# Normalised attention and a low-rank mixer on one core: the first batch staged by neighbouring heads, with 64x64 turnings and another written order

## The chip, the cores and the metric

The kernel runs on one core of a Trainium2 chip, as one program. The metric is the device time in microseconds (us) of one execution. Five engines work beside each other, each through its own list of instructions in a fixed order: TensorE (PE; its weight loads are shown apart as PEld), VectorE (DVE), ScalarE (ACT), GpSimd (POOL) and SyncE (SP), which here only issues transfers. An instruction starts when the one before it on its engine lets it, and when the semaphores that it waits for have come.

## What is computed

There are 8 batches of 12 heads, 448 positions and 64 numbers per head, and a two-layer mixer with 768 columns and a hidden width of 3072. Cut to what matters:

```
q_n, k_n = rmsnorm(q, g_q), rmsnorm(k, g_k)          # x / sqrt(mean(x*x) + 1e-6) * g
scores   = q_n @ k_n.T / sqrt(64)
attn     = exp(scores - max) / (sum + 1e-9)
x        = (attn @ v) laid out as [batch, 448, 768]
h        = x.T @ U @ V                               # rank 32, over the positions
u        = x + h.T
out      = u + relu(u @ w_ch1) @ w_ch2
```

All inputs and the output are float32; the kernel multiplies in bfloat16.

## The kernel before, in words

**Tiling.** The 12 heads of a batch are worked in three groups of four heads, so there are 24 groups (`groups`, L76). The 448 positions are cut into 7 blocks of 64 (`NT`). A group's queries and keys lie in SBUF as `qf` and `kf`, 128 partitions by 14 rows of 64 numbers: two heads share the partitions (64 each), and the index c = 0, 1 in the free direction gives the other two. A pair of heads is worked together through the scores, their exponentials and the products with the values; a batch has six pairs.

**Norms.** For each group the squares of `qf` and `kf` are taken (ACT or POOL), summed on DVE into `ssq`, and turned into reciprocal roots on ACT by a logarithm and an exponential (`rs`, or `rp` where the result goes to PSUM for DVE). A multiplication by them on DVE or POOL gives `qn` and `kp` in bfloat16.

**Turning.** The scores need queries and keys with the 64 numbers of a head on the partitions. In groups 0 to 5 TensorE does it, seven 128x128 transposes for q and seven for k (`turn`, L363), into PSUM tiles `pt`. `take_q` (L371) copies a pair's queries to `qT` times the gain `gg`; `take_k` (L380) copies the keys to `kT` in three copies: 128x384 for the first six blocks and two of 64x64 for the last. `kT` has 512 columns; in its last 128 the two heads' keys stand in a diagonal of 64x64 blocks with zeros beside them (`fill_keys`, L260), so that one matmul gives the last scores of both heads. From group 6 on, DMA transposes do this.

**Pairs.** In most groups a pair is heads 0 and 2, or 1 and 3, of the group, which is how a whole 128x128 transpose leaves them. Only group 2 (`BESIDE`, L83) is loaded so that neighbours make a pair; each of its q and k loads is then two transfers of 64 partitions (L97).

**Scores, exponentials, products.** For a pair, `scores` (L418) fills four tiles: three of 128x896 (two heads by 448) and one of 128x448, from a pool of two PSUM buffers. `exps` (L433) turns each into `E` on ACT. `products` (L490) multiplies E with the values for half of the rows, and `norms` (L507) divides on DVE into `x`.

**Mixer.** `mix_t0` and `mix` (L644, L654) add the low-rank part of batch 0 and turn it to `uT`. `up_one` (L706, matmuls on L711) makes the first four tiles of the hidden layer in single steps, `up` (L689, matmuls on L693) the others, six matmuls each, `down` (L733, matmuls on L740) the second layer. The weights come in float32 from HBM and are cast to bfloat16 by POOL's transfers: `w1b` in four pieces (hidden tiles 0 to 3, 4 to 9, 10 to 15, 16 to 23; L295) and `w2b` in eight (L303).

**The order.** The first batch is ordered by hand: the string `FRONT` (L897) names steps in the order in which they are put into the engines' lists. A step is a short name with its numbers, and after a colon the engine (a for ACT, v for DVE, p for POOL). `S.0.1` is score tile 1 of pair 0, `E.0.1` its exponential, `V.0.1` the products of its second half, `N` the division, `turn`, `tq` and `tk` the turning and the copies, `sq`, `sm`, `rt`, `sc` the four steps of the norms, `val` the casting of a group's values (after it stands `load` of the group three later), `w` one piece of weights, `b.22` 22 matmuls on an identity whose result nobody uses (`keep_busy`, L242; 72 of them stand at the very start), `mt`, `mtc`, `mix`, `mc` and `u` the mixer. Before, the first norms of group 0 go in two parts of three or four blocks (`sqp`, `smp`, `rt0`, `scp`; `PARTS` are blocks 0 to 3 and 4 to 6). Behind the front, a planner (L1050) mixes the attention of the later batches with the mixer by estimated costs that begin at zero there.

**Transfers.** SP's list of loads begins with q and k of groups 0 and 1, q of group 2, v of group 0, k of group 2, v of group 1, then U, V, v of group 2. In the built program each transfer of SP and ACT waits for the landing of the one eight places earlier in their common order. POOL's transfers, the weights, are a queue of their own.

**Buffers.** The small PSUM tiles (`pt`, `rp`, `pv`, `busy`, `pu`, `ph`, `pg`) share four buffers; a step that takes one waits for the last reader of the tile that was there.

Of the kernel before, what the change touches and what calls it, by code (L numbers as in the profile page):

```python
# [9 lines left out]
FP32 = mybir.dt.float32  # L10
BF16 = mybir.dt.bfloat16
# [16 lines left out]
def kernel(  # L28
# [19 lines left out]
    P = 128  # L48
# [34 lines left out]
    BESIDE = 2  # L83
# [22 lines left out]
    def load_v(gi, eng=None):  # L106
        b, h0, n = groups[gi]
        t = staged[gi][2]
        toks = v[b, h0:h0 + n].rearrange("h (p j) d -> p h (j d)", j=NT)
        for i in range(2):  # L110
            (eng or nc.sync).dma_start(
                t[i * R:(i + 1) * R, :NM, :].rearrange("p (h j) d -> p h (j d)", j=NJ),
                toks[:, :, i * NJ * D:(i + 1) * NJ * D])
        for e in range(2):
            hs = slice(e, 4, 2) if gi == BESIDE else slice(2 * e, 2 * e + 2)
            (eng or nc.sync).dma_start(t[e * R:(e + 1) * R, NM:, :], toks[:, hs, 2 * NJ * D:])
# [30 lines left out]
    def squares_part(i, lo, hi, eng):  # L147
        if (0, i) not in sqs:
            sqs[(0, i)] = normp.tile([P, 2 * NT, D], FP32, name="sq", tag="sq")
        sq, x = by_c(sqs[(0, i)])[:, :, lo:hi, :], by_c(staged[0][i])[:, :, lo:hi, :]  # L150
        if eng is None:
            nc.scalar.activation(sq, x, AF.Square)
        else:
            eng.tensor_mul(sq, x, x)

    def sums_part(i, lo, hi):
        nc.vector.tensor_reduce(ssqs[0][:, i, :].rearrange("p (c j) -> p c j", c=2)[:, :, lo:hi],
                                by_c(sqs[(0, i)])[:, :, lo:hi, :], AX, ALU.add)

    def scale_part(i, lo, hi, eng):  # L160
        eng.tensor_tensor(
            normed[0][i].rearrange("p j c d -> p c j d")[:, :, lo:hi, :], by_c(staged[0][i])[:, :, lo:hi, :],
            rss[0][:, i].rearrange("p (c j) -> p c j ()", c=2)[:, :, lo:hi, :].to_broadcast([P, 2, hi - lo, D]),
            ALU.mult)
# [61 lines left out]
    PARTS = ((0, 4), (4, NT))  # L226
    for i in range(2):
        load_qk(0, i)
# [5 lines left out]
    load_qk(2, 0)  # L234
    load_v(0)
    load_qk(2, 1)
# [29 lines left out]
    fill_keys(0, nc.vector)  # L266
    for e in range(2):
        nc.gpsimd.tensor_mul(gp[:, e * D:(e + 1) * D], grow[:, 0, :], grow[:, 1, :])
# [76 lines left out]
    def fill_mixer():  # L345
        nc.gpsimd.memset(Uz, 0.0)
        fill_values(2, nc.gpsimd)
        fill_keys(1, nc.gpsimd)
# [14 lines left out]
    def turn(gi, i):  # L363

        pt = pts[(gi, i)] = ps.tile([P, NT, 2, R], BF16, name="pt", tag="ps")
        pos = POS_ODD if i == 0 and groups[gi][0] % 2 else POS
        for j in (*range(*PARTS[1]), *range(*PARTS[0])) if gi == 0 else range(NT):
            nc.tensor.transpose(pt[:, pos[j]].rearrange("p a r -> p (a r)"),  # L368
                                normed[gi][i][:, j].rearrange("p c d -> p (c d)"), ident)

    def take_q(gi, a, scalar=False):  # L371
        qT = q_bufs[gi % 2][:, a]
        dst, src = qT.rearrange("p (j r) -> p j r", r=R), pts[(gi, 0)][:, :, a, :]
# [6 lines left out]
    def take_k(gi, a):  # L380
        src = pts[(gi, 1)][:, :, a, :]
        kT = kT_bufs[gi % 2][:, a]
        nc.vector.tensor_copy(kT[:, :SM].rearrange("p (j r) -> p j r", r=R), src[:, :2 * NJ])
# [106 lines left out]
    def products(b, pr, half):  # L490
# [4 lines left out]
        first_h, step = (2 * lp, 1) if gi == BESIDE else (lp, 2)  # L495
# [11 lines left out]
    def norms(b, pr, half):  # L507
        gi, lp = divmod(b * NPAIR + pr, 2)
        first_h, step = (2 * lp, 1) if gi == BESIDE else (lp, 2)
# [360 lines left out]
    for b in range(B):  # L870
# [36 lines left out]
        u.2.1 V.5.1 N.5.0 rt.3 u.3.0 u.3.1 N.5.1 u.0.3 u.1.3 u.2.3 u.3.3 mt.3 u.0.2 mix.4 mtc.3 u.1.2 mix.5 mc.4:a u.2.2 u.3.2  # L907
        mc.5:a u.0.4 u.1.4 u.2.4 u.3.4 u.0.5 u.1.5 u.2.5 u.3.5
# [4 lines left out]
    def square_of(gi, i, eng):  # L913
        eng = None if eng is nc.scalar else eng
        squares(gi, i, eng, beside if (gi, i) == (2, 0) else None)

    placed = {t.partition(":")[0]: t.partition(":")[2] for t in FRONT.split()}
    rps = {}

    def root_of(gi, i, name):  # L920
        if placed.get(name) != "v":
            return rss[gi][:, i]
        if gi not in rps:
            rps[gi] = ps.tile([P, 2, 2 * NT], FP32, name="rp", tag="ps")
        return rps[gi][:, i]

    def part(t, p):
        lo, hi = PARTS[p]
        return t.rearrange("p (c j) -> p c j", c=2)[:, :, lo:hi]

    def roots_in(gi):
        if gi not in rss:
            rss[gi] = normp.tile([P, 2, 2 * NT], FP32, name="rs", tag="rs")
        return rss[gi]

    def log_part(i, p):
        nc.scalar.activation(part(roots_in(0)[:, i], p), part(ssqs[0][:, i], p), AF.Ln, scale=1.0 / D, bias=eps)

    def root_part(i, p):
        nc.scalar.activation(part(root_of(0, i, f"scp.{i}.{p}"), p), part(rss[0][:, i], p), AF.Exp, scale=-0.5)  # L940

    def log_of(gi, i=None):
        h = slice(0, 2) if i is None else slice(i, i + 1)
        nc.scalar.activation(roots_in(gi)[:, h], ssqs[gi][:, h], AF.Ln, scale=1.0 / D, bias=eps)

    def root(gi, i=None):
        if i is None and placed.get(f"sc.{gi}.0") == placed.get(f"sc.{gi}.1"):
            root_of(gi, 0, f"sc.{gi}.0")
            dst = rss[gi] if gi not in rps else rps[gi]
            nc.scalar.activation(dst, rss[gi], AF.Exp, scale=-0.5)  # L950
            return
        for i in range(2) if i is None else (i,):
            nc.scalar.activation(root_of(gi, i, f"sc.{gi}.{i}"), rss[gi][:, i], AF.Exp, scale=-0.5)

    def scale_by(gi, i, eng, lo=0, hi=NT):
        rs = rps[gi] if eng is nc.vector else rss[gi]
        eng.tensor_tensor(
            normed[gi][i].rearrange("p j c d -> p c j d")[:, :, lo:hi, :],
            rs[:, i].rearrange("p (c j) -> p c j ()", c=2)[:, :, lo:hi, :].to_broadcast([P, 2, hi - lo, D]),
            by_c(staged[gi][i])[:, :, lo:hi, :], ALU.mult)  # L960

    steps = {
        "sqp": lambda i, p, eng: squares_part(i, *PARTS[p], None if eng is nc.scalar else eng),
        "smp": lambda i, p, eng: sums_part(i, *PARTS[p]),
        "rt0": lambda i, p, eng: (log_part(i, p), root_part(i, p)),
        "ms": lambda eng: fill_mixer(),
        "scp": lambda i, p, eng: scale_by(0, i, eng, *PARTS[p]),
# [4 lines left out]
        "turn": lambda gi, i, eng: turn(gi, i),  # L972
# [3 lines left out]
        "sm": lambda gi, i, eng: sums(gi, i),  # L976
        "rt": lambda gi, *a: (log_of(gi, *a[:-1]), root(gi, *a[:-1])),
        "sc": lambda gi, i, eng: scale_by(gi, i, eng),
# [141 lines left out]
```

## Time and profile before

| what | value |
|---|---|
| median of 3 runs | 570.82 us (570.54 to 720.74) |
| the profiled execution | 570.46 us |
| its span, first to last instruction | 568.7 us, so 1.8 us lie around it |
| busy PE / ACT / POOL / DVE | 561.5 / 308.5 / 204.5 / 189.4 us |
| granted TensorE clock | 0.999 |

Busy time by stretch (us from the span's start), from the windows view:

| stretch | PE | of it unused matmuls (L245) | ACT | DVE | POOL |
|---|---|---|---|---|---|
| 0 to 12 | 10.25 | 8.42 | 6.72 | 7.05 | 7.60 |
| 12 to 33 | 19.30 | 2.72 | 20.79 | 18.27 | 18.42 |
| 33 to 40 | 7.00 | 0 | 3.17 | 4.33 | 4.37 |
| 40 to 90 | 49.76 | 0 | 33.90 | 27.33 | 30.55 |

Matmuls overlap, so a busy PE is not a PE at its peak: 72 matmuls may show 5.73 us while one alone shows 0.35. To get what one costs in a row of equal ones, the start of the next group minus the start of this is divided by the count. Landing times in this text are an issue's start plus its time to landing.

### The profile page before, as it was taken

What the parts mean: (1) busy time and instruction counts of PE and PEld (TensorE: products, weight loads), DVE (VectorE), ACT (ScalarE), POOL (GpSimd) and SP (SyncE); (2) the same over time, 40 slices, a digit from 0 to 9 for tenths busy, and PEclk for the clock granted to TensorE, in tenths of its full rate; (3) what the DMA queues carried; (4) which work ended last, traced back from release to release, by engine and by line L of the source; (5) the groups of instructions that cost most, each with busy time, mean ns of one, the idle gap of its engine ahead of it and who ended that gap; (6) DMA issues with size and microseconds to landing.
All of it is one profiled execution on the core that took longest, in us unless ns stands there. A gap on an engine that the chain in (4) does not pass through costs nothing.

```text
span 568.7 us, 11567 instructions
## 1 busy us (share of the span) xinstructions
PE 561.5 (99%) x4756; PEld 321.9 (57%) x4756; DVE 189.4 (33%) x425; ACT 308.5 (54%) x518; POOL 204.5 (36%) x308
## 2 busy tenths in 40 slices
PE   8899999999999999999999999999999999999997
PEld 7665555555555555555556555565465555555555
DVE  6955564312443222521235231532034210410011
ACT  6967760888454776287553677367752544014300
POOL 6874784355332724343522532351531000000000
PEclk9999999999999999999999999999999999999999
DMA  9999999784247633595335735375215200320022
GB/s 241 223 242 240 247 228 179 159 225 114 62 91 171 170 98 63 90 233 144 74 96 107 203 90 125 67 204 128 36 33 86 56 23 0 77 56 0 1 57 56
DMA packets 104830, 68.20 MB, mean 120 GB/s; under 512 B 66633, under 2 KB 100937, under 8 KB 104777
## 3 DMA queue, kind: packets, MB, share of 16 engines
q1 hardware_dynamic: 95124, 57.83, 44.2%
q0 software_dynamic: 9408, 9.44, 10.0%
q8 instruction: 37, 0.61, 0.5%
q10 hardware_dynamic: 244, 0.20, 0.1%
q14 instruction: 17, 0.13, 0.1%
HBM read 52.20 MB, written 11.01 MB: 111 GB/s over the span
## 4 chain that ended last, share of the span: by engine, by line
PE 94%; ACT 4%; DMA 1%; DVE 0%; POOL 0%; issue 0%; POOLq 0%
PE po L740 38%; PE ph L693 37%; PE pv L541 4%; ACT E L435 3%; PE sc L464 2%; PE sl L455 2%; PE sl L476 2%; PE pr L568 1%; PE po L727 1%; PE pv L537 1%; PE sc L430 1%; PE sc L711 1%; PE sc L626 1%; PE pu L609 1%; DMA ob<-in_g_k_dram 1%; PE pt L368 1%
## 5 line engine op out<-in xcount | busy, mean ns | idle before, releaser
L693 PE MATMUL ph<-uT,w1b 128*128 128x448 bf16 x1128 | 223.9, 352 | 0.0
L740 PE MATMUL po<-w2b,hT 128*128 128x384 bf16 x1296 | 223.5, 326 | 0.0
L740 PEld LDWEIGHTS <-hT 128*128 128x128 bf16 x1296 | 122.8, 98 | 84.1 <-issue 7.0
L693 PEld LDWEIGHTS <-w1b 128*128 128x128 bf16 x1128 | 108.2, 98 | 97.6 <-issue 2.2
L700 ACT ACTIVATE hT<-ph 128x448 bf16<-128x448 f32 x187 | 99.7, 550 | 106.9 <-PE ph L693 106.5
L399 POOL TENSOR_SCALAR qT<-qT,gg 128x448 bf16<-128x448 bf16 x36 | 50.4, 1402 | 92.4 <-DMA qT<-qn 77.3
L457 ACT ACTIVATE E<-sl,gg 128x448 bf16<-128x448 f32 x72 | 41.6, 630 | 76.2 <-PE sl L455 75.3
L198 POOL TENSOR_TENSOR qn<-qf,rs 128x384 bf16<-128x384 f32 x36 | 29.9, 830 | 111.9 <-ACT rs L175 106.1
L468 ACT ACTIVATE E<-sc,gg 128x896 bf16<-128x896 f32 x72 | 68.9, 1019 | 0.0
L750 DVE TENSOR_TENSOR ob<-po,x 128x384 f32<-128x384 f32 x46 | 25.6, 557 | 103.7 <-PE po L740 103.0
L167 DVE TENSOR_REDUCE ssq<-sq 128x14 f32<-128x896 f32 x45 | 47.0, 1078 | 23.9 <-ACT sq L141 23.2
L545 DVE RECIPROCAL r<-pv 128x6 f32<-128x6 f32 x42 | 8.2, 195 | 125.4 <-PE pv L541 125.1
L435 ACT ACTIVATE E<-sc,gg 128x896 bf16<-128x896 f32 (+1 forms) x42 | 37.0, 951 | 1.1 <-PE sc L430 0.7
L541 PE MATMUL pv<-va,E 128*128 128x65 bf16 x756 | 35.4, 194 | 0.0
L541 PEld LDWEIGHTS <-E 128*128 128x128 bf16 x756 | 32.4, 98 | 3.2
L198 POOL TENSOR_TENSOR kp<-kf,rs 128x384 bf16<-128x384 f32 x36 | 29.8, 828 | 0.0
L537 PE MATMUL pv<-vl,E 128*128 128x130 bf16 x126 | 27.6, 219 | 0.0
L633 DVE TENSOR_TENSOR x<-sc,x 128x384 bf16<-128x384 f32 x42 | 20.8, 550 | 17.4 <-PE sc L626 17.4
L546 DVE TENSOR_TENSOR x<-pv,r 128x384 bf16<-128x384 f32 x42 | 23.4, 557 | 1.4
L174 ACT ACTIVATE rs<-ssq,eps 128x28 f32<-128x28 f32 x20 | 6.3, 315 | 32.1 <-DVE ssq L167 32.1
L477 ACT ACTIVATE E<-sl,gg 128x448 bf16<-128x448 f32 x36 | 23.3, 646 | 0.0
L206 POOL CAST va<-vf 128x768 bf16<-128x768 f32 x24 | 20.7, 862 | 0.2 <-DMA vf<-in_v_dram 0.2
(130 smaller groups left out, 426.4 us busy)
## 6 DMA issues: line engine op xcount, KB each, us to landing
qf<-in_q_dram SPq DMA_DIRECT2D x23, 448.0 KB, 3.7
kf<-in_k_dram SPq DMA_DIRECT2D x23, 448.0 KB, 4.9
vf<-in_v_dram SPq DMA_DIRECT2D x48, 192.0 KB, 5.5
out_dram<-ob SPq DMA_DIRECT2D x48, 192.0 KB, 2.7
w2b<-in_moe_w_ch_dram POOLq DMA_DIRECT2D x8, 576.0 KB, 15.3
w1b<-in_moe_w_ch_dram POOLq DMA_DIRECT2D x2, 1152.0 KB, 17.6
vf<-in_v_dram SPq DMA_DIRECT2D x48, 32.0 KB, 5.1
w1b<-in_moe_w_ch_dram POOLq DMA_DIRECT2D x1, 1536.0 KB, 28.5
```

The costliest lines, as they stand in the source:

```text
L167: nc.vector.tensor_reduce(ssqs[gi][:, i, :], sqs.pop((gi, i)), AX, ALU.add)
L198: nc.gpsimd.tensor_tensor(main.rearrange("p (t i) d -> p i t d", i=2), src[:, c, :2 * NJ].rearrange("p (i t) d -> p i t d", i=2), rs[:, c, ...
L399: nc.gpsimd.tensor_scalar(qT[:, a], qT[:, a], gg[:, 0:1], None, ALU.mult)
L435: nc.scalar.activation(es[(b, pr)][:, 2 * r:2 * r + n, :], sc[:, :n, :S], AF.Exp, scale=scal, bias=bias)
L457: nc.scalar.activation(E[:, 4 + i, :], ts[i], AF.Exp, scale=scal, bias=bias)
L468: nc.scalar.activation(E[:, 2 * r:2 * r + 2, :], tiles[r][:, :, :S], AF.Exp, scale=scal, bias=bias)
L537: nc.tensor.matmul(pv[:, i].rearrange("p e d -> p (e d)"), E[:, 2 * NJ, w:w + P], vl[:, lp, :], start=True, stop=False)
L541: nc.tensor.matmul(pv[:, i, e, :], E[:, 2 * j + e, w:w + P], va[:, (lp + 2 * e) * NJ + j, :], start=False, stop=(e == 1 and j == NJ - 1))
L693: nc.tensor.matmul(ph, w1b[:, dt, ht * P:(ht + 1) * P], uT[:, dt, off:off + S], start=(dt == 0), stop=(dt == KD - 1))
L700: nc.scalar.activation(hT[:, ht, off:off + S], ph, AF.Relu)
L740: nc.tensor.matmul(po, hT[:, ht, col:col + P], w2b[:, ht, half * HALF:(half + 1) * HALF], start=(ht == 0), stop=(ht == KH - 1))
L750: nc.vector.tensor_tensor(ob[:, h], po, urows(b, col, half), ALU.add)
```

## The change

All three groups of the first batch (`EARLY = 3`) are worked by pairs of neighbouring heads. Group 0 is loaded in four transfers of 224 KB (q of heads 0 and 1, k of them, q of heads 2 and 3, k of them) in place of two of 448 KB; groups 1 and 2 in plain transfers of 128 partitions, so group 2's two pairs of 64-partition transfers become two whole ones. The values of group 0 are loaded ahead of q and k of group 2. Group 0 and 1 do their norms by halves of seven rows (one pair of heads), group 2 squares and scales whole tensors.

`turn_half` turns one pair's q or k: 14 transposes of 64x64 blocks (16 for k, two of them of zeros, which put the diagonal with its zeros into PSUM), where `turn` had seven of 128x128 for both pairs. So a group takes 60 transposes in place of 14. `take_k` is then one copy of 128x512. The product of the gains moves from POOL to DVE, the filling of the second `kT` from POOL to DVE. The unused matmuls in `FRONT` become 60 instead of 76. On ACT the copy `tq.0.0` moves to DVE, and three halves of squares stand ahead of the first exponential besides those of group 0. Pieces of `w1b` are issued at other places of the order: the first stands behind both squares of group 2 on POOL.

In the built program the number of matmuls grows by 122 (138 more transposes, 16 fewer unused ones). Behind the front the order on every engine is the same as before: on ACT from the ReLU of the first hidden tiles on, on PE from the last `u` steps on, on POOL from the squares of k in group 3 on.

The core of the diff:

```
-    BESIDE = 2
+    EARLY = 3
...
-        if gi == BESIDE:
-            for a in range(2):
-                nc.sync.dma_start(staged[gi][i][a * R:(a + 1) * R].rearrange("p (c j) d -> p c (j d)", c=2),
-                                  (q, k)[i][b, h0 + 2 * a:h0 + 2 * a + 2].rearrange("c (p j) d -> p c (j d)", j=NT))
-            return
...
+    def load_half(i, c):
+        nc.sync.dma_start(staged[0][i][:, c * NT:(c + 1) * NT].rearrange("p j d -> p (j d)"),
+                          (q, k)[i][0, 2 * c:2 * c + 2].rearrange("a (p j) d -> (a p) (j d)", j=NT))
...
+    def squares_half(gi, i, c, eng):
...
+    def sums_half(gi, i, c):
+        nc.vector.tensor_reduce(cut(ssqs[gi][:, i], c), cut(sqs[(gi, i)], c), AX, ALU.add)
...
-    for i in range(2):
-        load_qk(0, i)
+    for c in range(2):
+        for i in range(2):
+            load_half(i, c)
...
-    load_qk(2, 0)
     load_v(0)
-    load_qk(2, 1)
+    for i in range(2):
+        load_qk(2, i)
     load_v(1)
...
-        for j in (*range(*PARTS[1]), *range(*PARTS[0])) if gi == 0 else range(NT):
+        for j in range(NT):
...
+    def turn_half(gi, i, c):
+        pt = pts[(gi, i, c)] = ps.tile([P, NT + i, R], BF16, name="pt", tag="ps")
+        for j in range(NT):
+            for a in range(2):
+                rows = slice(a * R, (a + 1) * R)
+                nc.tensor.transpose(pt[rows, POS[j] + (a if i and j == 2 * NJ else 0)], normed[gi][i][rows, j, c], ident[rows, rows])
+                if i and j == 2 * NJ:
+                    nc.tensor.transpose(pt[rows, POS[j] + 1 - a], Vr[rows, S:], ident[rows, rows])
...
     def take_k(gi, a):
-        src = pts[(gi, 1)][:, :, a, :]
         kT = kT_bufs[gi % 2][:, a]
+        if gi < EARLY:
+            nc.vector.tensor_copy(kT.rearrange("p (j r) -> p j r", r=R), pts[(gi, 1, a)])
+            return
...
     FRONT = """
-        sqp.0.1:a sqp.0.0:p gr smp.0.1 sqp.1.1:a sqp.1.0:p smp.0.0 rt0.0.1 smp.1.1 gains:p smp.1.0 rt0.1.1 pg rt0.0.0 b.22
-        scp.0.1:v scp.1.1:p rt0.1.0 scp.0.0:v sq.1.0:a scp.1.0:p gg turn.0.0 sm.1.0 ms tq.0.0:a turn.0.1 b.17 w tk.0.0 rt.1.0
-        sq.1.1:a tq.0.1:v S.0.1 sc.1.0:v S.0.0 b.13 sq.2.0:p E.0.0 sm.1.1 turn.1.0 E.0.1 S.0.2 val.0 tk.0.1 E.0.2 tq.1.0:v b.5
-        sm.2.0 S.0.3 b.8 E.0.3 S.1.0 rt.1.1 tq.1.1:v sq.2.1:p S.1.1 V.0.1 E.1.0 sc.1.1:v b.7 E.1.1 S.1.2 turn.1.1 sm.2.1 E.1.2
-        S.1.3 V.0.0 tk.1.0 val.1 E.1.3 N.0.1 rt.2 tk.1.1 sc.2.0:p sc.2.1:v S.2.0 V.1.0 E.2.0 S.2.1 prepu N.1.0 E.2.1 S.2.2
-        N.0.0 V.1.1 w E.2.2 turn.2.1 N.1.1 prepv S.2.3 b.4 tk.2.0 E.2.3 S.3.0 E.3.0 tk.2.1 S.3.1 w turn.2.0 V.2.0 E.3.1 tq.2.1:v
-        S.3.2 N.2.0 mt.0 E.3.2 tq.2.0:v S.3.3 V.2.1 val.2 mtc.0 E.3.3 S.4.0 N.2.1 E.4.0 S.4.1 V.3.1 w V.3.0 E.4.1 N.3.1 S.4.2
-        mix.1 N.3.0 E.4.2 S.4.3 sq.3.0:p mt.1 mc.1:v E.4.3 S.5.0 mtc.1 E.5.0 S.5.1 V.4.0 sq.3.1:p V.4.1 E.5.1 N.4.0 S.5.2 mix.0
-        N.4.1 E.5.2 S.5.3 mix.2 mc.0:v mix.3 E.5.3 sm.3.0 u.0.0 mc.2:a u.1.0 mt.2 mc.3:a u.0.1 u.1.1 mtc.2 V.5.0 sm.3.1 u.2.0
...
+        sq.0.0.0:a gm:v sq.0.1.0:a gr b.10 sm.0.0.0 gains:p sq.0.0.1:a sm.0.1.0 pg rt.0.0.0 sq.0.1.1:p b.19 sm.0.0.1 rt.0.1.0
+        sc.0.0.0:v rt.0.0.1 sc.0.1.0:p sq.1.0.0:a sm.0.1.1 turn.0.0.0 sq.1.0.1:p gg turn.0.1.0 rt.0.1.1 tq.0.0:v b.10 sq.1.1.0:a
+        tk.0.0 sc.0.1.1:p sm.1.0.0 sq.1.1.1:a S.0.0 sc.0.0.1:p sm.1.1.0 E.0.0 turn.0.1.1 sm.1.1.1 S.0.1 rtc.1.0 turn.0.0.1
+        sm.1.0.1 val.0 E.0.1 S.0.2 sc.1.1.0:v b.8 sc.1.0.0:v E.0.2 turn.1.1.0 tk.0.1 S.0.3 sq.2.0:p b.7 rtc.1.1 tq.0.1:v tk.1.0
+        S.1.0 E.0.3 sc.1.1.1:v b.6 E.1.0 S.1.1 sq.2.1:p sm.2.0 turn.1.0.0 E.1.1 S.1.2 tq.1.0:v turn.1.1.1 E.1.2 w sm.2.1 S.1.3
+        V.0.0 V.0.1 E.1.3 sc.1.0.1:p tk.1.1 S.2.0 rt.2 N.0.0 S.2.1 V.1.1 E.2.0 val.1 N.0.1 turn.1.0.1 sc.2.1:v E.2.1 S.2.2 V.1.0
+        tq.1.1:v E.2.2 S.2.3 N.1.0 turn.2.1.1 w sc.2.0:v E.2.3 S.3.0 turn.2.1.0 ms E.3.0 S.3.1 tk.2.0 turn.2.0.0 E.3.1 prepv
+        S.3.2 tq.2.0:v V.2.0 N.1.1 E.3.2 V.2.1 tk.2.1 S.3.3 val.2 turn.2.0.1 N.2.1 E.3.3 S.4.0 N.2.0 S.4.1 E.4.0 V.3.1 tq.2.1:v
+        w V.3.0 N.3.1 E.4.1 S.4.2 prepu N.3.0 E.4.2 sq.3.0:p mt.0 S.4.3 mt.1 mtc.0 E.4.3 S.5.0 mtc.1 mix.1 w E.5.0 sm.3.0 S.5.1
+        V.4.0 sq.3.1:p E.5.1 S.5.2 mc.1:v V.4.1 N.4.0 E.5.2 S.5.3 mix.3 N.4.1 mix.2 E.5.3 sm.3.1 u.0.1 mt.2 mc.2:a V.5.0 mc.3:a
+        V.5.1 mtc.2 rt.3 N.5.0 u.1.1 u.0.2 u.1.2 N.5.1 mix.0 u.0.3 mt.3 mc.0:a u.1.3 mix.4 mtc.3 mix.5 mc.4:a u.0.0 u.1.0 mc.5:a
...
     """
```

`rt.g.i.c` and `rtc.g.c` are the roots of one half (`roots_of`): a logarithm and an exponential on ACT, with a second exponential where q and k are scaled by different engines.

More of the change, by code (lines that the diff above doesn't have):

```diff
@@ L144, in squares, with cut @@
             eng.tensor_mul(sq, staged[gi][i], staged[gi][i])
[L147 to L151, printed above, removed]
+    def cut(t, c):
+        return t[:, c * NT:(c + 1) * NT]
+    def squares_half(gi, i, c, eng):
+        if (gi, i) not in sqs:
+            sqs[(gi, i)] = normp.tile([P, 2 * NT, D], FP32, name="sq", tag="sq")
+        sq, x = cut(sqs[(gi, i)], c), cut(staged[gi][i], c)
+        if eng is nc.scalar:
             nc.scalar.activation(sq, x, AF.Square)
@@ L265, with product_gains @@
         fill_values(i, nc.vector)
-    fill_keys(0, nc.vector)
-    for e in range(2):
-        nc.gpsimd.tensor_mul(gp[:, e * D:(e + 1) * D], grow[:, 0, :], grow[:, 1, :])
+    for i in range(2):
+        fill_keys(i, nc.vector)
+    def product_gains(eng):
+        for e in range(2):
+            eng.tensor_mul(gp[:, e * D:(e + 1) * D], grow[:, 0, :], grow[:, 1, :])
     gg = consts.tile([P, 2], FP32)
@@ L927, in part, with square_of, name_of, roots_of @@
[L927 to L931, printed above, removed]
+    def square_of(gi, i, *a):
+        c, eng = a[:-1], a[-1]
+        if c:
+            squares_half(gi, i, *c, eng)
+        else:
+            squares(gi, i, None if eng is nc.scalar else eng, beside if (gi, i) == (2, 0) else None)
+    roots_at = {}
+    def name_of(gi, i, c):
+        return f"sc.{gi}.{i}" if c is None else f"sc.{gi}.{i}.{c}"
+    def roots_of(gi, which, c):
@@ L932, in roots_in @@
         if gi not in rss:
             rss[gi] = normp.tile([P, 2, 2 * NT], FP32, name="rs", tag="rs")
[L934 to L960, printed above, removed]
+        cols = slice(0, 2 * NT) if c is None else slice(c * NT, (c + 1) * NT)
@@ new lines, in roots_of @@
+        lo, hi = which[0], which[-1] + 1
+        nc.scalar.activation(rss[gi][:, lo:hi, cols], ssqs[gi][:, lo:hi, cols], AF.Ln, scale=1.0 / D, bias=eps)
+        by_vector = [i for i in which if placed[name_of(gi, i, c)] == "v"]
+        rp = ps.tile([P, 2, 2 * NT], FP32, name="rp", tag="ps") if by_vector else None
+        for i in which:
+            roots_at[(gi, i, c)] = (rp if i in by_vector else rss[gi])[:, i, cols]
+        if len(by_vector) in (0, len(which)):
+            nc.scalar.activation((rp if by_vector else rss[gi])[:, lo:hi, cols], rss[gi][:, lo:hi, cols], AF.Exp, scale=-0.5)
+        else:
+            for i in which:
+                nc.scalar.activation(roots_at[(gi, i, c)], rss[gi][:, i, cols], AF.Exp, scale=-0.5)
@@ L971 @@
         "gg": lambda eng: nc.vector.tensor_copy(gg, pgs[0]),
-        "turn": lambda gi, i, eng: turn(gi, i),
+        "turn": lambda gi, i, c, eng: turn_half(gi, i, c),
         "tq": lambda gi, a, eng: take_q(gi, a, eng is nc.scalar),
```

55 lines of the change are left out of this document (22 added, 33 removed).

## Prediction

> **What bounds the kernel now.** I read the page first, then the chain in order of time, then ACT's and PE's timelines up to 80 us, then the landings of the weights. The page says that TensorE is at work in every slice but the first and last:
>
> ```profile
> span 568.7 us, 11567 instructions
> PE 561.5 (99%) x4756; PEld 321.9 (57%) x4756; DVE 189.4 (33%) x425; ACT 308.5 (54%) x518; POOL 204.5 (36%) x308
> ```
>
> Behind the front the order is unchanged on every engine, so what the change can move is the moment at which PE enters that part: the first `up` matmul on L693. The chain (start, length, what) shows what sets it:
>
> ```profile
> 9.50 0.58 PE pt L368 x7
> ...
> 11.17 0.93 ACT sq L141
> 12.10 3.22 ACT E L435 x4
> ...
> 20.52 5.71 ACT E L435 x7
> 26.23 0.04 issue
> 26.27 3.34 ACT E L435 x4
> 29.61 0.04 issue
> 29.66 0.36 PE sc L430 x2
> ...
> 37.73 1.89 PE sc L711 x10
> 39.62 1.14 PE ph L693 x6
> ```
>
> From 12 to 29.6 us it is ACT with the exponentials, then PE without a gap. The ACT timeline (start, length, instruction) shows how little is idle between:
>
> ```profile
> 11.17 0.93 ACT L141 ACTIVATE sq<-kf 128x896 f32<-128x896 f32 x1
> 12.01 3.31 ACT L435 ACTIVATE E<-sc,gg 128x896 bf16<-128x896 f32 x4
> 15.20 0.32 ACT L944 ACTIVATE rs<-ssq,eps 128x14 f32<-128x14 f32 x1
> 15.54 0.19 ACT L953 ACTIVATE rp<-rs 128x14 f32<-128x14 f32 x1
> 15.66 3.31 ACT L435 ACTIVATE E<-sc,gg 128x896 bf16<-128x896 f32 x4
> 18.85 0.33 ACT L944 ACTIVATE rs<-ssq,eps 128x28 f32<-128x28 f32 x1
> ...
> 19.43 13.55 ACT L435 ACTIVATE E<-sc,gg 128x896 bf16<-128x896 f32 x16
> ```
>
> Four exponentials (one pair) take 3.19 (12.01 to 15.20); a group of roots between them 0.46 (15.20 to 15.66) or, with three instructions, 0.58 (18.85 to 19.43). Six pairs and both groups are 20.18; the stretch from 12.01 to 32.88 is 20.87, so 0.69 is lost to waits, all of it in the last four pairs (13.45 against 12.76). So ACT can end earlier only by beginning earlier.
>
> **The start of the exponentials.** The new order needs half of q and k for the first pair, but PE's list holds the unused matmuls ahead of the first turning. The 72 end where `pg` starts, at 7.02. Then 10 more at 62 ns (17 of them from 10.29 to 11.34) are 0.62; the two `pg` 0.68 (0.37 from 7.02, 0.31 from 7.68); 19 more 1.18: 9.50. Before, the first turning began at 9.50 too. The data are ready by then: halves of q and k have at most the landing of the whole ones (4.33 and 5.55); two squares of 448 (0.55, between 0.52 for 384 and 0.93 for 896) end at 4.9, sums (0.61 by the line from 0.55 for 384 to 1.08 for 896) at 5.9, roots at 6.5, the scaling of q on DVE near 7.0 and of k on POOL (0.94, between 0.83 and 1.05) at 7.5. The norms by halves, the gain product on DVE and the earlier loads are thus covered by 2 us of unused matmuls; without these they would be worth up to that.
>
> A 64x64 transpose is not in the trace. The nearest rows are 24 ns (L568, 64 columns of weights, 16 in 0.38), 31 ns (L541, 65 moving columns, 6 in 0.19) and 56 ns (L368, 128x128, 14 in 0.78). I take 30, ends 24 and 56. Then 14 blocks take 0.42 and q can be copied from 10.1 (with 0.17 of latency); 16 for k end at 10.55. The copy of k is 128x512: 0.35 for 384 and 0.45 for 448 with a gain bound it loosely; I take 0.42 (0.35 to 0.55): 11.0. The next 10 unused matmuls end at 11.02. Scores 0.36 and handing over: the first exponential at 11.45, 0.55 ahead of 12.01. The copy saves DVE about 0.25 of the old 0.68 (10.59 to 11.27), six times, which ACT's 20 us of exponentials hide.
>
> **The stream.** Among the exponentials there are now three groups of roots, not two: one more of 0.46. The squares of group 1 lie ahead of the stream, in ACT's waits between 7 and 11.4. I keep the 0.69 of waits (ends 0 and 1.2; where I follow the buffers, S.3.0, S.3.3 and S.4.0 come 0.1 to 0.2 late, as turnings and products stand ahead of them). So the stream ends 0.55 - 0.46 = 0.1 earlier.
>
> **PE behind the stream.** From S.5.3 at 31.74 to L693 at 39.46 PE is full: 7.72. The new order has the same steps there and `mix.0` as well (32.09 to 32.48, 0.39), which stood ahead of S.5.3. So +0.39. In the stream itself PE has, from S.2.0 (18.58) to S.5.3 (13.16 us), 16 score tiles 4.2, 8 products 4.0, two `mt` 0.9, one `mix` 0.4 and five turnings of 74 blocks 2.2: 11.7, and some 0.1 per turning for changing the shape (scores beside 128-wide work take 0.30 where two take 0.19 in a row). That fits, with 1 us to spare. Other moved fillings, casts and divisions are on DVE and POOL, which the buffers let be up to 1 us late; the exponentials hide them.
>
> Together: 39.46 - 0.1 + 0.39 = 39.75, **+0.3 us**, ends -0.8 (no waits, 24 ns) and +2.
>
> **The weights.** The first piece of `w1b` was issued at 11.24. Now it stands behind both squares of group 2 on POOL; these need q and k of group 2, which I put at 13 to 14.5 (the last bytes of k landed at 15.3 before, with one more group of values ahead now and the weights gone), so with two squares of 1.7 the issue is near 17. SP's queue has eight transfers in flight; with the small U loads among them it may leave the engines partly idle near 15 to 17. The landings before, piece 2 and then pieces 3 and 4 in turn:
>
> ```profile
> DMA to landing us min/median/max: 14.3/14.3/14.3
> ...
> DMA to landing us min/median/max: 21.0/21.0/21.0
> ...
> DMA to landing us min/median/max: 28.5/28.5/28.5
> ```
>
> Issued at 22.55, 24.54 and 26.76 they landed at 36.9, 45.5 and 55.3; piece 1 took 9.9. Now piece 1 lands near 17 + 9.9 = 26.9 (wanted at 32), and piece 2, issued near 20 behind it, 8.7 (piece 3's time, same size) to 14.3 (its own) later: 35.6 to 41.2. I take 39.5, since the same loads of groups 3 and 4 run beside it, somewhat advanced. It is wanted at 39.75, so it just comes. Pieces 3 and 4 are wanted at 49.3 and 60.6, the fourth `w2b` piece (landed 77.8) at 79.3: 1.5 us or more to spare.
>
> Against the profiled execution: 570.46 + 0.3 = 570.8; the median of the runs is 570.82, 0.36 above that execution, so I say **571.0 us**: no change that can be told.
>
> **The rivals.**
>
> *The weights come late (slower).* Piece 2 lands after PE wants it; it decides from 39.75 on. For it: the page's DMA row stands at 9 through its first seven slices (100 us) and the issue is 6 us later; against it: SP's loads have run ahead. At 41.2 PE waits 1.45: 572.4; if piece 1 is itself slower by 1, 573.4.
>
> *Turnings are dear (slower).* At 56 ns, 74 blocks are 1.9 more and PE's 11.7 + 0.5 becomes 14.1 against 13.2: it binds the stream, by 0.9 to 1.9; I take 1.4: 572.4. Against it are the 24 ns of L568, which also has 64-wide weights. The Trainium skill (TensorEngine Tiling (Array Packing), Restrictions) says that column tiling excludes Fast Weight Load, and TensorE: Matmul & The Clock Gate (LDWEIGHTS) gives columns / 1.2 ns: by my estimate 53 ns for a block, unless two halves of the array load at once; by that the time is this rival's. The row with 64-wide weights speaks against the rule binding.
>
> *The clock drops (slower, small).* With 16 fewer unused matmuls, PE could lose its clock for a few us near 10 to 14; the granted clock was 1.00 there with PE idle for up to a fifth. A stretch of 3.4 us at half speed costs up to 1.7: 572.7. The Trainium skill (TensorE: Matmul & The Clock Gate, Part 4: PE-mode transpose) says that transposes do not count as activity as matmuls do; with 42 of them no run here shows that.
>
> *Earlier (faster).* The waits of 0.69 go: -0.1 - 0.69 + 0.39 = -0.4; with blocks at 24 ns and the short copy 0.3 more at the start: 570.82 - 0.7 = 570.1. For it: the new order was spread by pairs; against it: one more group of roots, three late score tiles.
>
> **How the numbers follow.** As forecast, 570.3 to 571.7: 0.48. Weights late: 0.20. Turnings dear: 0.12. Clock: 0.03. Earlier: 0.17. The range for 8 in 10 is 569.4 to 573.3. All cases lie within 2% (11.4 us, about what a measurement of this kernel can tell from no change): 0.97; 0.01 faster and 0.02 slower are left for what I have not seen.
>
> **What would show it.** Right: first turning at 9.5, first exponential near 11.4, three groups of roots on ACT, S.5.3 near 31.6, L693 at 39.5 to 40. Wrong: a PE wait on a transfer ahead of L693; blocks above 45 ns; a first turning well ahead of 9.5, which would mean that the unused matmuls run faster than I count; a granted clock below 1 after 5 us.

## The result and the profile after

The changed kernel takes 575.67 us (median of six runs, 574.02 to 576.87) against 571.52 for the kernel before on the same chip: a ratio of **1.0073, 95% interval 1.0047 to 1.0099**. One of the six executions of the kernel before took 720.74 us, and the ratio leaves it out. By the 2% that the forecast uses for a change that can be told this is no change. But the interval excludes 1, and 575.67 lies outside the predicted range of 569.4 to 573.3.

The page of the profiled execution (576.87 us; the spans of the six runs are 572.2 to 575.1):

```profile
span 575.1 us, 11802 instructions
PE 565.8 (98%) x4878; PEld 324.9 (56%) x4878; DVE 188.6 (33%) x420; ACT 309.7 (54%) x520; POOL 203.7 (35%) x305
...
PEclk9979999999999999999999999999999999999999
```

The third digit of the clock row, 29 to 43 us, is a 7 (before, all are 9). The chain of waits, up to the first `up` matmul (now L705, before L693):

```profile
4.41 7.71 DMA vf<-in_v_dram
...
12.13 6.21 DMA vf<-in_v_dram
...
18.78 1.06 POOL w1b L293
...
21.43 9.41 DMA qf<-in_q_dram
...
30.94 0.32 POOL Ub L340
31.25 0.24 POOL x L341
...
31.55 1.04 PE pu L660 x4
...
46.00 1.13 PE ph L705 x6
```

Before, the chain between 12 and 29.6 us was ACT with its exponentials. Now it is transfers, then POOL with a cast of U (`Ub`), then PE. On the timeline the first L705 begins at 45.84 where L693 began at 39.46: 6.38 us later, against a span longer by 6.4 (575.1 - 568.7). So the whole loss of this execution lies ahead of that matmul; the part behind has kept its length, as the forecast assumed. ACT's timeline shows where it is lost:

```profile
12.01 1.01 ACT L447 ACTIVATE E<-sc,gg 128x896 bf16<-128x896 f32 x1 [0.41 <-PE sc L442]
...
20.00 0.32 ACT L945 ACTIVATE rs<-ssq,eps 128x28 f32<-128x28 f32 x1 [0.47 <-DVE ssq L162]
20.48 9.49 ACT L447 ACTIVATE E<-sc,gg 128x896 bf16<-128x896 f32 x11
32.99 0.63 ACT L447 ACTIVATE E<-sc,gg 128x448 bf16<-128x448 f32 x1 [3.02 <-PE sc L442]
```

The first exponential comes at 12.01, exactly as before, not at 11.45. The exponentials from the third pair on, behind the roots of group 2, begin 1.05 later (20.48 against 19.43). Then, at 30, ACT stands still for 3.02 because PE does. PE's waits from 12 to 50 us, and POOL's timeline, which ends the longest of them:

```profile
PE pu L660 <- POOL x L341: 2.6, 1, 2.6
```

```profile
27.19 0.83 POOL L201 CAST va<-vf 128x768 bf16<-128x768 f32 x1 [1.72 <-DMA vf<-in_v_dram]
29.04 0.29 POOL L203 CAST vl<-vf 64x128 bf16<-64x128 f32 x1 [1.03 <-DMA vf<-in_v_dram]
29.62 0.29 POOL L203 CAST vl<-vf 64x128 bf16<-64x128 f32 x1 [0.29 <-DMA vf<-in_v_dram]
30.07 0.82 POOL L293 DMA_DIRECT2D w1b<-in_moe_w_ch_dram  x1 [0.16 <-issue]
30.94 0.32 POOL L340 CAST Ub<-x 128x160 bf16<-128x160 f32 x1
31.20 0.29 POOL L341 CAST x<-x 128x128 bf16<-128x128 f32 x1
```

POOL waits three times for the values of group 2; the casts of U (`prepu`) stand behind them in its list, and `mt.0` on PE needs these. In the kernel before they ran at 22.05, ahead of the values. The values themselves are late: they landed between 25 and 26 before (the last two issued from 19.91 on, 5.2 to landing), at 29.6 now. The windows (busy time of PE, PEld, DVE, ACT, POOL; granted clock, DMA share, GB/s) of before show full transfers:

```profile
15.00:20.00 5.00, 4.04 (x65) 2.85 (x62) 4.85 (x12) 4.94 (x11) 3.11 (x5) 1.00 1.20 213
```

and those of after:

```profile
15.00:20.00 5.00, 4.43 (x82) 3.12 (x80) 3.83 (x8) 4.50 (x10) 3.66 (x4) 1.00 0.28 56
...
30.00:35.00 5.00, 3.45 (x16) 1.79 (x16) 1.57 (x3) 1.24 (x2) 3.79 (x5) 0.57 1.12 256
35.00:40.00 5.00, 5.00 (x75) 3.69 (x74) 3.49 (x9) 4.06 (x7) 3.41 (x4) 0.75 1.15 224
```

Two things are to be read here. From 15 to 20 us the DMA engines are at 0.28 in place of 1.20, a hole worth some 4 us of full transfers (5 times 0.92, by 1.15). SP did not fill it: behind a small load of U that it had issued by 15.4, its next issue came at 17.05, when k of group 2, eight places earlier in its list, had landed (7.58 and 9.4), and this one and the next were the last loads of U and V. And behind PE's wait its clock is 0.57 and 0.75: (1 - 0.57) x 5 + (1 - 0.75) x 5 = 3.4 us, about 6.8 us at half speed.

### The profile page after: what moved, and what is told of

It reads as the page before. It is cut to its first block, busy times and chain, and to the rows that moved or that the text cites. A ratio compares the mean times of both kernels' runs of the same rounds, so it can differ in the third digit from the quotient of the medians.

```text
span 575.1 us, 11802 instructions
## 1 busy us (share of the span) xinstructions
PE 565.8 (98%) x4878; PEld 324.9 (56%) x4878; DVE 188.6 (33%) x420; ACT 309.7 (54%) x520; POOL 203.7 (35%) x305
## 4 chain that ended last, share of the span: by engine, by line
PE 94%; DMA 4%; SPq 1%; POOL 1%; ACT 0%; issue 0%; DVE 0%; POOLq 0%
PE po L752 37%; PE ph L705 37%; PE pv L553 4%; DMA vf<-in_v_dram 2%; PE sc L476 2%; PE sl L467 2%; DMA qf<-in_q_dram 2%; PE sl L488 2%; PE pr L580 1%; PE po L739 1%; PE pv L549 1%; PE sc L442 1%; PE sc L723 1%; PE sc L638 1%; PE pu L621 1%; PE pt L365 0%
## 5 line engine op out<-in xcount | busy, mean ns | idle before, releaser
L705 PE MATMUL ph<-uT,w1b 128*128 128x448 bf16 x1128 | 223.9, 352 | 0.0
L705 PEld LDWEIGHTS <-w1b 128*128 128x128 bf16 x1128 | 108.2, 98 | 97.7 <-issue 2.2
L762 DVE TENSOR_TENSOR ob<-po,x 128x384 f32<-128x384 f32 x46 | 25.7, 558 | 103.7 <-PE po L752 103.0
L162 DVE TENSOR_REDUCE ssq<-sq 128x14 f32<-128x896 f32 x43 | 44.9, 1079 | 24.9 <-ACT sq L140 23.2
L553 PEld LDWEIGHTS <-E 128*128 128x128 bf16 x756 | 32.4, 98 | 3.2
```

Of the source, the lines that this page charges most:

```text
L162: nc.vector.tensor_reduce(ssqs[gi][:, i, :], sqs.pop((gi, i)), AX, ALU.add)
L553: nc.tensor.matmul(pv[:, i, e, :], E[:, 2 * j + e, w:w + P], va[:, (lp + 2 * e) * NJ + j, :], start=False, stop=(e == 1 and j == NJ - 1))
L705: nc.tensor.matmul(ph, w1b[:, dt, ht * P:(ht + 1) * P], uT[:, dt, off:off + S], start=(dt == 0), stop=(dt == KD - 1))
L762: nc.vector.tensor_tensor(ob[:, h], po, urows(b, col, half), ALU.add)
```

## The experiments

The pieces of `w1b` turn out to be what matters. In this table the issue times are those of the profiled executions, a ratio is taken against the kernel before on the same chip (it is not the quotient of the two medians), and "casts" means that the casts of U stand ahead of group 2's values.

| kernel | first, second piece at (us) | other edits | ratio, 95% interval |
|---|---|---|---|
| before | 11.2, 22.6 | | 1 |
| after | 18.8, 22.1 | | 1.0073 (1.0047 to 1.0099) |
| e1 | 19.0, 22.4 | casts | 1.0073 (1.0051 to 1.0096) |
| e2 | 18.5, 21.8 | unused matmuls in the wait | 1.0057 (1.0037 to 1.0076) |
| e3 | 11.3, 20.3 | | 1.0082 (1.0053 to 1.0110) |
| e4 | 11.1, 19.4 | casts | 1.0088 (1.0058 to 1.0118) |
| e5 | 18.0, 21.3 | casts, sums late | 1.0062 (1.0037 to 1.0087) |
| e6 | 11.3, 26.0 | | 1.0010 (0.9990 to 1.0031) |
| e7 | 18.1, 21.5 | values ahead of U, V | 1.0132 (1.0112 to 1.0152) |
| e9 | 11.4, 28.0 | casts | 1.0024 (1.0009 to 1.0039) |
| e10 | 10.9, 19.2 | casts, sums late | 1.0031 (1.0007 to 1.0055) |
| e11 | 11.8, 27.1 | casts, earlier start | 1.0027 (1.0006 to 1.0047) |
| e12 | 18.4, 25.7 | casts | 1.0047 (1.0022 to 1.0071) |
| e14 | 13.0, 27.1 | casts, sums late | 1.0019 (1.0004 to 1.0034) |
| e16 | 11.0, 21.0 | | 1.0029 (1.0002 to 1.0056) |
| e18 | 11.5, 21.4 | casts | 1.0014 (0.9994 to 1.0033) |
| e8 | 17.9, 22.6 | on the kernel before | 1.0077 (1.0051 to 1.0102) |
| e13 | 11.2, 19.4 | on the kernel before | 1.0042 (1.0024 to 1.0060) |
| e15 | 17.2, 23.8 | on the kernel before | 1.0036 (1.0019 to 1.0054) |
| e17 | 11.2, 24.7 | on the kernel before | 1.0027 (1.0007 to 1.0047) |

**First theory: PE's wait for the casts, and the clock behind it.** Four kernels.

e1 moves the casts of U up:

```
-  ... turn.2.0.0 E.3.1 prepv
+  ... turn.2.0.0 E.3.1 prepv prepu
-  w V.3.0 N.3.1 E.4.1 S.4.2 prepu N.3.0
+  w V.3.0 N.3.1 E.4.1 S.4.2 N.3.0
```

> The two casts of U (prepu) stand directly behind prepv on POOL, ahead of the casts of group 2's values; nothing else is changed. Theory (TensorE's wait of 2.62 us at mt.0 for these casts, and the clock lost behind it, are the loss): the wait at L660 is under 0.5 us, the granted clock stays at 1.0 from 28 to 38 us, the first up matmul comes at 40 to 41 instead of 45.84, and the time is 570.0 to 571.5. Rival A (the late pieces of w1b set the entry): still 574.5 or more. Rival B (the clock drops for another reason, fewer unused matmuls or more turnings): the wait goes, the half clock stays, 572.5 to 573.5.

Measured: 575.25, nothing won. The wait at L660 for the casts is gone, but another has come. PE's waits of 20 to 50 us and DVE's timeline:

```profile
PE ph L669 <- DVE uT L678: 1.8, 1, 1.8
```

```profile
33.67 1.09 DVE L162 TENSOR_REDUCE ssq<-sq 128x14 f32<-128x896 f32 x1 [2.86 <-POOL sq L143]
34.67 0.61 DVE L678 CAST uT<-ph 128x448 bf16<-128x448 f32 x1
```

DVE stands 2.86 us in front of the sums of group 3 (`sm.3.0`). They wait for POOL's squares, and these for q of group 3, which is late too; the copy of `uT` that PE needs stands behind them. So the first theory, that the casts' place is the loss, falls. Rival A gave the number, but not the reason: no piece of weights was waited for.

e2 puts `b.40` ahead of `mt.0`.

> 40 unused matmuls ahead of mt.0 fill TensorE's wait (40 times 62 ns are 2.5 us); the casts stay where they are. Theory (the wait costs 2.6 and the half clock behind it about 3): the clock stays at 1.0, mt.0 still begins near 31.5, the first up matmul at 42.5 to 43.2, 572 to 573. If the clock has nothing to do with the wait: 575.5 as before.

Measured: 574.63; the clock is 0.999 or 1.0 in all four executions, where `after` has 0.994 to 1.0, and L705 comes at 43.6. This fits a low clock that follows from PE's wait, though three of the six executions of `after` kept 0.999 or 1.0 as well; holding it up saves some 1 us at most in the median, since the wait itself stays.

e3 moves the first piece up, e4 does this and e1's edit:

```
-  sm.1.0.1 val.0 E.0.1 ... turn.1.1.1 E.1.2 w sm.2.1 S.1.3
+  sm.1.0.1 w val.0 E.0.1 ... turn.1.1.1 E.1.2 sm.2.1 S.1.3
```

> The first piece of w1b is issued ahead of val.0 on POOL (near 12 to 13 us) and not behind the squares of group 2 (18.78). Theory (the transfers' hole from 15 to 20 us makes group 2's values late, and these hold the casts of U): the values land near 27 to 28.5 instead of 29.9, the wait at mt.0 falls to 0.5 to 1.5, 571 to 573.5. Rival (the values are late because SP issues them late, whatever the weights do): they land at 29.5 to 30 still, 575 to 576. If the piece takes the transfers from q and k of group 2, rt.2 comes later and the stream of exponentials ends up to 1.5 us later.

> Both edits: the casts of U ahead of the values' casts, and the first piece of w1b ahead of val.0. Theory: no wait at mt.0, the stream of exponentials ends no later than with the casts alone: 569.5 to 571.0. If the casts alone are all: as with the casts alone, within 0.5.

Measured: 575.66 and 576.05. The hole is filled (a DMA share of 1.20 from 15 to 20 us in e3), and still nothing is won. The second piece, which had followed POOL's list, came earlier too (20.3 and 19.4), and q of group 3 landed at 31.7 in e3 (21.41 and 10.3), about as in `after` (32.4). PE waits 2.5 us at L660 in e3, and in e4 4.2 at L669 for the copy of `uT`.

**Second theory: two queues hold PE behind late transfers.** e5 mends both, POOL's (as e1) and DVE's:

```
-  E.5.0 sm.3.0 S.5.1 ... N.4.1 mix.2 E.5.3 sm.3.1 u.0.1
+  E.5.0 S.5.1 ... N.4.1 sm.3.0 mix.2 E.5.3 u.0.1
-  mtc.2 rt.3 N.5.0 ... mt.3 mc.0:a u.1.3
+  mtc.2 N.5.0 ... mt.3 mc.0:a sm.3.1 rt.3 u.1.3
```

> Second theory: two queues hold TensorE behind late transfers, POOL (casts of U behind group 2's values) and, when that is mended, DVE (the sums of group 3's squares ahead of the copy of uT, 1.82 us of waiting with the casts ahead, 4.18 with the piece early as well). Here the casts of U stand behind prepv, and the two sums and the roots of group 3 stand later (behind N.4.1 and behind mc.0), so that nothing that TensorE needs stands behind group 3's transfers. Second theory: no wait of TensorE above 0.5 us between 20 and 45 us, clock 1.0, first up matmul at 40.3 to 41.3, 570.5 to 572. Rival (the transfers themselves are needed, whatever the queues): another wait of 1.5 us or more shows up, 573.5 or more.

Measured: 575.49. In the profiled execution the forecast for the front is nearly right (L705 at 41.0, clock 1.0, one wait of 0.8 at L669 where at most 0.5 was expected). But the time is given back where nobody looked, far behind the front (PE's waits from 40 us on):

```profile
PE po L752 <- DMA w2b<-in_moe_w_ch_dram: 1.3, 1, 1.3
```

PE now reaches the second layer before its weights do. The hole is still there (0.35 from 15 to 18 us), and I take what was not transferred in it to be missing at the end. That execution was also the fastest of five (573.52), so the median says it better: mending the queues alone recovers nothing that can be told.

**Third theory: room in the transfers.** e6 leaves the queues as they are and spaces the pieces; it is e3 and

```
-  N.1.0 turn.2.1.1 w sc.2.0:v ... E.3.1 prepv
+  N.1.0 turn.2.1.1 sc.2.0:v ... E.3.1 prepv w
```

> The order of the queues is that of the changed kernel, but the first piece of w1b is issued ahead of val.0 (11.1 us) and the second behind prepv (25 to 26 us, instead of 22.12), so that group 2's values and group 3's q and k have the transfers nearly for themselves from 22 on. If the weights' competition is what makes them late: the values land at 25 to 27, q of group 3 at 28 to 30, the wait at mt.0 is under 0.7, that for the copy of uT under 0.7, 570.5 to 572.5. If the loads are late by SP's own list: waits of 2 us or more stay, 574 or more.

Measured: **572.25, ratio 1.0010 (0.9990 to 1.0031)**. Against e3 only the second piece has moved, from 20.3 to 26.0, and the loss is gone. q of group 3, issued at 21.41 in e3 and at 21.38 here, lands at 28.7 and not at 31.7; its time to landing in e3 and in e6:

```profile
DMA to landing us min/median/max: 10.3/10.3/10.3
...
DMA to landing us min/median/max: 7.3/7.3/7.3
```

Only 1.2 us of the wait at L660 are left:

```profile
PE pu L660 <- POOL x L341: 1.2, 1, 1.2
```

e8 is the reverse, the kernel before with its first piece late:

```
-  tq.0.0:a turn.0.1 b.17 w tk.0.0 ... sq.2.1:p S.1.1
+  tq.0.0:a turn.0.1 b.17 tk.0.0 ... sq.2.1:p w S.1.1
```

> The kernel before, with its first piece of w1b issued behind the second square of group 2 on POOL (near 18 to 19 us, as in the changed kernel) instead of at 11.24. If the lateness alone costs the time: 573.5 to 575.5. Second theory (lateness costs only with the changed queues, since the kernel before has the casts of U ahead of the values and the sums of group 3 late): 570.5 to 572.

Measured: 575.3, ratio 1.0077. With nothing else of the change, the kernel before loses as much as the change does. The second theory had said that its queues would protect it. They don't (PE's waits, and DVE's from 26 to 40 us):

```profile
PE pu L648 <- DVE x L514: 2.5, 2, 2.2
```

```profile
DVE ssq L167 <- POOL sq L144: 3.0, 2, 1.9
```

Here too it is group 3's sums, waiting for late q and k, with the divisions (`x`, L514) behind them. The hole is there as well (DMA share 0.33 from 15 to 20).

e7 loads the values of group 2 ahead of U and V.

> The values of group 2 are loaded ahead of U and V on SP's queue, nothing else. If the hole in the transfers (15 to 20 us) is there because the small loads of U stand in the list ahead of large ones: the hole is filled, the values land by 24 instead of 29.9, the casts of U come at 26 to 27.5, and the wait at mt.0 goes; the wait for group 3's squares (1 to 2 us) comes in its place: 572 to 574. If the values' landing does not matter: 575 or more.

Measured: 578.9, a miss in sign. The values land near 20 and the hole is smaller (a DMA share of 1.02 from 15 to 18 us, 0.58 from 18 to 21), but now V (issued at 20.38) comes behind the first piece of weights; POOL waits 7.35 us for it at `prepv`, the casts of U behind that run at 34.1, and PE waits 6.3. So group 2's values are not the point in themselves: whichever load rides beside the pieces comes late, and what stands behind it decides.

e12 keeps the hole and moves the second piece back; e10 fills the hole, keeps the second piece early and mends the queues.

> The first piece stays behind the squares of group 2 (18.8 us, the hole stays), but the second piece is issued behind prepv and the casts of U (near 26 instead of 22.12). So the loads have less beside them, and the weights are later by 4 us than in the kernel before. Third theory: the values land at 25.5 to 27.5, TensorE waits less than 1 us ahead of the first up matmul, but then for weights (second piece of w1b, or w2b) by 0.5 to 2: 571.5 to 573.5. If only the competition costs: 570.5 to 571.5. If only the hole: 574.5 or more.

> The queues mended (casts of U early, group 3's sums late) and the first piece early, so that the hole is filled; the second piece stays early (19.4) beside the loads. Third theory: with the hole filled the weights are not late at the end (no wait for w2b, which was 1.3 us with the queues alone), and with the queues mended late values hold nobody up: 570.5 to 572. If the second piece's competition costs the time in itself, whatever waits behind it: 574 or more.

Measured: 574.29 (1.0047) and 573.25 (1.0031). In e12 a late first piece costs time even with the second out of the way, and not by late weights, as I had expected: PE waits 2.1 at L669, for q of group 3 lands 10.8 after its issue, now beside the first piece. So the hole and the company of a piece are two sides of one move, and these runs don't part them; that bytes are missing afterwards shows as a wait for `w2b` of 1.3 in e5, 0.6 in e8 and 0.4 in e15 (and of 0.2 in e17, without a hole); e10, where the hole is filled, has none. My range for e10 was too low, as PE still waits 1.4 in two parts at L669 for `x` on DVE.

e10 says more beside e4 than beside e5: it is e4 with group 3's sums and roots later, and nothing else. Its ratio is 1.0031 (1.0007 to 1.0055) where e4 has 1.0088 (1.0058 to 1.0118), on another chip, though q of group 3 lands nearly as late (11.7 after its issue; 13.0 in e4) and the second piece is as early. PE's wait of 4.2 at L669 has become 1.4. So a load that comes late costs its time through the list behind it, and the second theory was half right: with the hole filled, mended queues recover most of the loss, as spacing the pieces does (e3 to e6); with the hole left (e5) they don't.

e13 and e15 ask the kernel before about the second piece:

> The kernel before, its second piece of w1b issued directly behind the values of group 1 (near 20.3 us instead of 22.55), so that it is in flight beside the values of group 2 and q and k of group 3. If two pieces beside these loads are what costs: the loads land 1 to 4 us later, 572 to 574. If 2 us of the second piece's issue matter little: 570.5 to 571.5.

> The kernel before with the first piece behind the second square of group 2 (18 us, so the hole is there) and the second behind the values of group 2 (27 us), directly ahead of the third. If the two pieces beside the loads were the cost of the run with the first piece late (575.3): 571 to 572.5, and no wait of TensorE above 1 us for the sums of group 3. If the hole is the cost: 574 or more; weights late: a wait for w1b or w2b in its place.

e13 puts `w` behind `val.1` instead of behind `V.1.1`; e15 is e8 without its `w` behind `V.1.1` and with one more behind `V.3.1`, so that the second piece goes at 23.8 (I had expected 27). Measured: 573.46 and 572.85. Three us earlier (19.4 in place of 22.6) costs 0.42%. A late first piece costs 0.36% where the second is late as well, and 0.77% where it isn't. e13's profiled execution was by chance one that lost nothing (570.56), so which wait costs the time there stays open.

e16 takes the changed kernel with `w` behind `ms`, near the kernel before's times (its second piece at 21.0, there at 22.6); e18 adds the casts.

> The changed kernel with the first piece ahead of val.0 (11.3 us) and the second behind the fillings (ms), near 22 us, as in the kernel before; the casts of U stay behind group 2's values. If the second piece's issue at 19.4 was what cost the time with the first piece early (575.7): 571.5 to 573.5, between that and the run with the second at 26 (572.25). If the loads need it later than 22: 574 or more.

> The run with the second piece at 22 us, and the casts of U behind prepv, ahead of group 2's values. That run still waited 1.0 us at mt.0 and gave 572.9. If the wait goes and nothing takes its place: 571 to 572. If the sums of group 3 on DVE, held by q of group 3, take its place: 572.5 to 574.

Measured: 572.93 (1.0029) and 572.38, **1.0014 (0.9994 to 1.0033)**. e18 is the change with its pieces and casts put back where they were in time, and it can't be told from the kernel before. In e16's profile q of group 3 (20.89) is issued ahead of the piece (20.98) and lands in 6.8 us; in e3, where the piece (20.33) goes ahead of it (21.41), in 10.3.

**In search of a better kernel.** e9 (e6 and the casts), e14 (e9 and e5's sums), e11 (e9 with `b.4` for `b.19` and for the second `b.10`, and the squares of k of group 1 behind `E.0.0`), and e17 (the kernel before, its second `w` behind `prepv`):

> The first piece of w1b ahead of val.0, the second behind prepv (as in the run with the pieces as before, which still waited 1.2 us at mt.0), and the casts of U ahead of that second piece and of group 2's values. Third theory (what the change lost was room in the transfers: a hole at 15 to 20 us, and then two pieces of weights beside the values of group 2 and the q and k of group 3): no wait of TensorE above 0.5 us, first up matmul at 40.2 to 40.8, 570.5 to 571.5. If the 1.2 us is only handed to the next wait: 572 to 573.

> The pieces spaced (11.3 and 28 us), the casts of U ahead of the second piece, and the sums and roots of group 3 later, so that neither POOL nor DVE holds TensorE for a late transfer. Theory: no wait of TensorE above 0.6 us before the first up matmul, which comes at 40.2 to 41.0; with the weights in time 570.3 to 571.3. If the weights are late then (second piece wanted near 40.5, landing 28 and 14 later): a wait of 1 to 2 us at L705, 571.5 to 573.

> As the kernel with pieces and casts, and an earlier start: 21 fewer unused matmuls ahead of the first scores (15 of 19, 6 of 10), and the two squares of k of group 1 behind the first exponential instead of ahead of it. First exponential at 10.2 to 10.6 instead of 11.8. If the stream of exponentials sets the entry: first up matmul 0.5 to 0.9 earlier, 569.7 to 570.8. If the q and k of group 2 (landing near 16.8) or the loads behind them set it: no gain, 570.5 to 571.5. If the clock drops in the first 15 us: up to 1.7 more.

> The kernel before with its second piece of w1b behind prepv (24.5 to 25 us) instead of 22.55. If the kernel before too loses a little, in some executions, to two pieces beside the loads: 570 to 571, and fewer executions above 571. If the second piece then comes late for the up part (wanted at 39.5; 24.7 and 14.3 are 39.0): 571.5 to 573.

Measured: 572.99, 573.02, 573.19 and 573.27; none beats the kernel before. That kernel loses when its second piece moves either way, to 19.4 (e13) or to 24.7 (e17). e14 and e11 show weights as the next bound: PE waits 0.6 and 0.5 at L705 for `w1b`, since the second piece is now late for it. e9's profiled execution was the slowest of twelve, with q of group 3 landing 10.3 after its issue and a wait of 2.2 at L669, though from 22.7 to 28.0 no piece was beside it; why is open. e11 has its first exponential at 10.09, 1.9 earlier than `after`, and pays for the missing unused matmuls with the clock:

```profile
12.00:15.00 3.00, 2.52 (x41) 1.75 (x40) 2.88 (x6) 2.75 (x6) 2.16 (x4) 0.50 1.09 273
15.00:18.00 3.00, 3.00 (x24) 1.62 (x24) 2.36 (x5) 2.15 (x6) 2.10 (x2) 0.50 1.25 200
```

Six us at half clock; the exponentials from the third pair on begin at 20.89, later than the 20.15 of e6.

## Why the prediction was wrong

**The step that failed** is the weights, and what I let stand on it. The prediction priced the moved first piece by its own landing alone: "piece 1 lands near 17 + 9.9 = 26.9", "piece 2 ... 39.5". Measured: issued at 18.78, as k of group 2 landed near 17.0 and not by 14.5, and landed at 30.7; piece 2 at 39.2, just in time for 39.75 as forecast, and PE never waited for a piece in that profile. What the piece does to the transfers beside it had no term: it was put at nothing. The runs show what it is worth: 0.77%, 4.4 us, when the first piece alone is moved in the kernel before (e8), and with the pieces early and apart the changed kernel is back at 0.10 to 0.14% (e6, e18). That the engines "may" be "partly idle near 15 to 17" was written and costed at nothing; the hole lasted from 15 to 20. The bytes missing from it then came as two pieces in flight beside group 2's values and group 3's q and k: q of group 3 took 11.0 us to land in place of some 6.4 (issued at 21.33, squared from 27.78). The Trainium skill (DMA: Bandwidth & Descriptors, Issuing engines are not separate DMA queues) says that transfers of all issuing engines run on the same 16 DMA engines and interleave; e3 against e6 agrees, where only POOL's piece moved and SP's loads gained 3 us.

**The sentence that hid it** is "Other moved fillings, casts and divisions are on DVE and POOL, which the buffers let be up to 1 us late; the exponentials hide them." I had not listed what stands behind each wait in POOL's list: `prepu` behind `val.2`, and on DVE the copy of `uT` behind `sm.3.0`. The cover is the exponentials only while PE feeds them; `mt.0` stands in PE's list ahead of the scores `S.4.3`, so the cover went with it. That mending these places recovered nothing while the first piece was late (e1, e5), and most of the loss once it was early (e10 against e4), shows that they are the paths on which late loads reach PE; the source is where the pieces stand.

**Point by point.** *Behind the front nothing moves:* right (6.38 of 6.4). *The start:* first turning 10.31, not 9.50, first exponential 12.01, not 11.45. The 82 unused matmuls ended at 8.62, not 7.64: from 3 to 6 us PE ran 31 of them, and 43 before, though the clock row says 1.00 both times; in e11 they ended at 7.53, so this varies between executions. The short copy is as forecast (0.42; measured 0.41). *Three groups of roots:* as forecast, 0.46 to 0.54 each, but the third also waits 0.47, because k of group 2 landed near 17.0, not by 14.5. *The clock:* it dropped, for twice the 3.4 us of the rival, but behind PE's wait and not at the start; that it can drop at the start with fewer unused matmuls, e11 shows. *Turnings dear:* excluded by the timeline of PE:

```profile
10.31 0.41 PE L373 MATMUL pt<-ident,qn 64*64 64x64 bf16 x14
10.56 0.39 PE L373 MATMUL pt<-ident,kp 64*64 64x64 bf16 x14
```

From one start to the next are 0.25 us for 14 blocks: 18 ns a block, below even the lower end of 24. My estimate of 53 from the Trainium skill's rules (TensorEngine Tiling (Array Packing), Restrictions; TensorE: Matmul & The Clock Gate, LDWEIGHTS) does not hold for these blocks. *The sum:* with the pieces and casts back in time (e18) the change costs 0.14% (-0.06 to 0.33), 0.8 us (-0.3 to 1.9), and e16, without the casts, 0.29%; the forecast for everything but the pieces was +0.3. *Weights late:* the right transfer, but in the profile of `after` the wrong victim; a wait for weights, of 0.2 to 1.3, shows in others (e5, e8, e11, e14, e15, e17).

## What to carry to other kernels

When a large transfer moves in the order, price it by the transfers around it, not by its own landing: look for the stretch that it leaves empty, and then for every load that will share the engines with it afterwards. Then go down each engine's list behind every instruction that waits for such a load, and write down who on the bottleneck engine needs what stands there. If taking away the first wait brings only the next one, look for the common source ahead of both; and test a mended list again once that source is gone, since one that recovers nothing alone may recover much then (e5 and e10).

## What was not expected of the hardware

The granted clock falls to half for some us after short waits of PE: a wait of 1.82 us in e1's execution was followed by 3.4 us at half clock, one of 2.62 in `after`'s by 6.8, one of 2.52 in e3's by none. By windows of 1 or 2 us, each low stretch comes to about 3.4 us of half clock (e1, e4, e9) or to twice that (`after`, e7, e11). The Trainium skill (TensorE: Matmul & The Clock Gate, Part 1) gives one idle window of about 3.4 us, freely running; the free running fits that one wait drops the clock and a like one doesn't, but here less than a whole window of waiting was enough. And a 64x64 transpose at 18 ns costs less than half of a 128x128 one (56): the 60 blocks of a group take 1.1 us, 14 whole ones 0.8.
